# Another order for TensorE, ScalarE and VectorE behind the opening of a fused attention and squared-ReLU kernel

## The chip, the cores and the metric

The kernel runs on one core of one Trainium2 chip. The metric is the device time of one execution in microseconds (us); the median of three executions stands for a version.

## The reference

Four batches of eight heads, 768 positions, 64 values a head. A query sees the 96 positions up to itself and the first 8 positions; the bias falls with the distance, by a slope for each head. The result goes through a layer with a squared ReLU.

```python
scores = scale * q @ k.T                       # per batch and head, 768 x 768
keep   = is_global | is_local                  # pos < 8, or 0 <= i - j < 96
scores = where(keep, scores - slope[h] * dist, -1e9)
a = softmax(scores);  o = a @ v                # (4, 8, 768, 64)
x = o.transpose(0, 2, 1, 3).reshape(3072, 512)
h = maximum(x @ w_in, 0)                       # w_in 512 x 2048
out = (h * h) @ w_out                          # w_out 2048 x 512, out 3072 x 512 f32
```

## The kernel before, in words

The 3072 rows are worked on in eight **halves** of 384 rows (half a batch each). For each half the kernel does, in tiles of 128 rows:

- loads of q, k and v by POOL (L396, cast to 16 bits on the way), and from the third half on a turn of q and k by DMA on SP's queue (`turn_by_dma`, L567);
- **scores** (`score_unit`, L610): matmuls with 64 rows for one or two tile pairs, two PSUM banks a unit; then the exponential on ScalarE (`ex`, L623) and the product with the mask of biases on VectorE (`phat`, L647);
- **attend** (L671): phat times v, with a column of ones that gives the sum; the normalisation on VectorE (`rec` L679, `tm` L681); and, from the third half on, a turn by DMA into `xt` (`to_x_by_dma`, L696, SP's queue), one for each of four pairs of heads;
- **layer 1**: x times w_in, plain (`layer1`, L717) or for some columns by a scheme with seven products in place of eight (`layer1_group`, L841), which needs sums of quarter matrices of x on VectorE (`x_mix`, L818) and keeps partial results (`kept`, L256 and L258; added to the product by L901); then the square (L924 on ScalarE; L926 and L760 on VectorE);
- **layer 2**: the squared rows times w_out, plain (`layer2`, L978) or in the same seven-product scheme for pairs of row tiles (`layer2_pair`, L1064), with sums of rows on VectorE (`mixed`, L1029), results handed out by `y` (L1126, L256, L258), and a store on SP's queue (L1149).

One half's attention is woven into the matrix products of the half before. No scheduler runs when the kernel is built: the table `ORDER` (from L52) is the order. A word names a job and its engine: `p` TensorE (by its number in TensorE's list), `a` ScalarE, `d` VectorE, `s` SP, `g` POOL, `l` a load on POOL's queue. The digits behind a point are the PSUM banks that the job takes, the number behind `+` is a filler, and `@` sets a load behind a DMA. `a` and `d` words name entries of one list of operations, so that writing `a596` as `d596` moves a copy from ScalarE to VectorE. `Plan.run` emits the words one after the other; each engine then works through its own words strictly in that order, and waits where an input, a bank or a buffer is not free:

```python
for word in ORDER.split():
    ...
    op = lists.get(word[0], self.rest)[int(word[1:])]
    self.now, self.spare = [int(i) for i in banks], int(spare or 0) / 100
    op.result = op.emit("POOL" if word[0] == "l" else self.LETTERS[word[0]])
```

Of the kernel before, what the change touches and what calls it, by code (L numbers as in the profile page):

```python
# [51 lines left out]
ORDER = """a4 d1 g2 p0.0 a6 s8 d12 a0 s10 d13 l3 l1 a18 l2 d15 d19 a26 d16 d3 l5 a30 d14 a20 a27 d9 l4 a23  # L52
d5 a22 d17 p1.12+31 a21 l0 p5.34 d11 a7 p10.56 l6 a28 p3 a24 l10 a31 d32 l9 a33 p6 d34 p4.7 a39
l7 p11 d37 a29 p9.0 p8.1 a46 l8 p2.23 d43 a40 p19.7 d35 l11 a47 p7 d55 a25 p13.51 d36 l13 a41
d44 p14.4 p12.67 d48 p15 a42 l12 d59 p17 a49 p16.0 p22.2 d45 l14 p24.4 a52 d51 p23.36 a50 d38
p34.50 l16 d58 a53 p21.7 d64 p25.2 a60 l18 p27.1 d65 a57 p20.4 a61 p32.37 d66 a81 d56 p31.2 l15
a73 p29.6 d68 p18.5 d72 p28.4 a74 p26.3 l19 p36.1 d54 a69 p35.2 p30.7 a86 d70 p33.54 d85 a71 d91
p39.16 a67 p40.27 a77 d63 p37.3 a82 d75 l17 a78 d62 p41.5 a92 d79 d76 p38.0 d84 d80 p45.4 d83
l21 a97 p48.1 d96 a101 l20 a98 p44.2 a89 p47.5 d107 l23 p46.7 a112 p42.0 d111 a108 d110 a93
p43.2 d109 p53.1 a87 p52.5 d102 p50.4 p49.7 a113 l22 d120 d100 a90 d105 p59.6 l27 a116 d119 a103  # L60
d106 p55.3 p51.1 l29 d94 a122 a88 d128 p65.2 l28 a104 d95 a117 p64.4 a118 p58.5 a129 a136 d114
p60.0 d99 a137 l30 d146 d191 p54.3 l24 p62.6 d115 d205 l25 p57.1 a133 p56.4 d125 d121 p63.7
p67.6 a123 d134 d135 a130 d206 p61.1 p72.3 a126 d132 p69.4 d189 a124 p77.7 a131 d156 p70.0 a142
p82.1 d157 d165 a159 p71.5 a160 p74.4 d162 l34 a166 d201 a163 p83.6 d147 a161 l26 p73.0 a167
d522 d164 a138 p84.3 l31 d158 d148 a168 a169 p79.52 d186 l35 a139 d202 p89.04 p81.1 d127 a198
l33 d151 p85 a187 d170 a178 d523 p86 a174 d207 a199 d184 p78.06 a179 d149 l32 p80.57 p88.41 d180
p87 a195 l36 d200 a175 p76.2 d203 a185 l37 d155 p75.4 a196 d193 p91.0 l38 a188 d143 s194 d197
p66.1 a181 l39 d172 a171 p95.3 d152 a173 p90.5 d223 p100.4 d153 a209 s224 a176 d236 p92 d204
p103.2 d177 d208 p68.3 d237 s216 a244 a140 d210 p93.6 d240 a211 p94 a182 d150 s217 a144 d219
p96.1 p104 d225 p97 d183 a245 d221 p98.7 s220 d239 a218 p102.3 d238 p111 d214 d228 s226 l44 p106  # L70
d222 d243 l43 d213 p109.61 s229 d227 p110.73 d154 p99 l40@217 a255 d258 s215 d141 p101 a256
l42@217 d145 a251 d272 d190 p113 l45 a252 a234 p114.73 d254 l41@217 d192 p108.61 p105.0 a248 l46
d246 a261 p107 d253 d259 a262 l47 d257 s260 p115.62 a249 s235 d230 p116.74 l48 p118.3 a264 d250
p131.1 a265 d232 d263 p117.6 a268 d231 a292 p122.2 d266 a273 p121.7 d233 a269 d212 p125.1 a271
d280 s324 p124 d284 p127.4 a283 p126 d241 a278 d267 p123.6 d285 a293 p137.1 s325 d281 p119.5
a287 p132 a286 p129.7 a279 d294 p130 p140 d323 a301 p142 d270 p134.6 a290 d274 a307 p128.1 a291
p135 d288 p133.2 a308 p136 d298 p141.5 a310 d300 s242 a299 p143.1 s282 a297 d309 p139 d326 p138
d524 p112 d395 l50@325 a305 s275 d311 p120 a303 l56 d306 a312 s289 d295 a302 p146.36 l53 p147.54
d304 p145.71 a330 s296 d313 l51@325 a333 p144.2 a331 d318 l52 p148.3 a334 d319 a276 l49@325
p149.5 d321 a327 a322 d433 d332 a328 l54 p151.64 p150.07 d314 p152 d320 a338 l57 d329 p159.1  # L80
a339 l55 p157.0 d336 a337 p172.7 a341 d340 p153 a352 d370 a342 p160.3 a350 d315 p169.6 s371 d353
a344 p158.7 p162 d351 p161 p154.4 d316 a355 d397 p166.3 a347 p164.7 d356 p163 s398 p156 d317
d358 d359 a366 p171.1 d343 p165 s399 p167 a360 d362 p181.7 a363 d335 a361 p170 d345 p175 d367
p177 a357 p174.0 d375 p173.5 a378 d373 p178.3 s247 s277 d369 p176 a383 s354 p180 d368 a372
p155.0 d349 a379 p168.1 a376 d382 a384 d400 p179 p183 l58@399 a364 p182.7 d380 a348 p184 s374
a377 l65 d385 p185.3 a389 l62 a387 d381 s386 p188.41 a365 d388 p187.05 l59@399 p186.27 a405
p189.6 d401 a409 l63 a413 d402 p190.0 a406 d416 l73 a410 d403 p191 a407 l61 d396 a414 p193.42
d412 a417 p194.65 l60@399 d411 a418 p192.71 p195 a422 d415 a419 l64 d391 p200.4 d429 a420 p206.7
d437 a426 p198.0 d392 p219.1 s438 d393 a434 d408 a427 p207.6 p204.4 d394 a447 s346 d489 p210
d443 a462 p202.5 a451 d428 p199.1 a423 d404 p211 a441 p213 d435 p197.4 p217.2 a432 d456 p205.5  # L90
s436 p218.1 d424 a444 d452 p196 d480 s491 a445 d476 a461 d460 p203.6 p215.7 d442 p223 a458 p221
d425 a453 p208 d421 s492 p209 d481 p220 a448 d483 p222.1 a469 d477 p214 a446 d467 p227.6 s390
# [1514 lines left out]
```

## Time and profile before

| | |
|---|---|
| three executions | 199.65, 199.69, 200.62 us; median 199.69 |
| profiled execution | 200.43 us, of which the span of instructions is 198.7 |
| TensorE | busy 191.6 us, 96% of the span, 2381 matmuls |
| weight loads | busy 163.2 us, 82% |
| VectorE | busy 176.3 us, 89%, 450 instructions |
| ScalarE | busy 151.0 us, 76%, 321 instructions |
| turns into xt by DMA | 24, from issue to landing 2.3 to 7.0 us, median 3.0 |
| granted TensorE clock | 1.00 |

In the profile PE is TensorE (PEld its weight loads), DVE VectorE, ACT ScalarE, SP and POOL the queues that issue DMAs; L671 is line 671 of the kernel. Times count from the start of the span. "x24" is a number of instructions, and the name behind an arrow in square brackets is what ended the idle time before the row. Rows of TensorE overlap, since a matmul's results are still draining when the next one streams.

### The profile page before, as it was taken

What the parts mean: (1) busy time and instruction counts of PE and PEld (TensorE: products, weight loads), DVE (VectorE), ACT (ScalarE), POOL (GpSimd) and SP (SyncE); (2) the same over time, 40 slices, a digit from 0 to 9 for tenths busy, and PEclk for the clock granted to TensorE, in tenths of its full rate; (3) what the DMA queues carried; (4) which work ended last, traced back from release to release, by engine and by line L of the source; (5) the groups of instructions that cost most, each with busy time, mean ns of one, the idle gap of its engine ahead of it and who ended that gap; (6) DMA issues with size and microseconds to landing.
All of it is one profiled execution on the core that took longest, in us unless ns stands there. A gap on an engine that the chain in (4) does not pass through costs nothing.

```text
span 198.7 us, 5980 instructions
## 1 busy us (share of the span) xinstructions
PE 191.6 (96%) x2381; PEld 163.2 (82%) x2381; DVE 176.3 (89%) x450; ACT 151.0 (76%) x321; POOL 66.9 (34%) x82
## 2 busy tenths in 40 slices
PE   7798999999999999999999999999999999999993
PEld 3576899856888687788888998999889999999993
DVE  7589696899999999999989999899899996978971
ACT  6799797899555888976999679878897578769211
POOL 8996565187108701940194007800000000000000
PEclk9999999999999999999999999999999999999999
DMA  5999999999999998999899799996531221201214
GB/s 152 182 150 194 189 180 172 209 195 155 182 192 92 155 205 218 107 127 145 218 118 153 104 222 129 161 175 147 102 102 37 94 57 40 109 0 53 109 53 158
DMA packets 106987, 27.52 MB, mean 139 GB/s; under 512 B 97104, under 2 KB 104016, under 8 KB 106960
## 3 DMA queue, kind: packets, MB, share of 16 engines
q0 software_dynamic: 74944, 13.11, 90.1%
q1 hardware_dynamic: 30816, 13.45, 31.7%
q10 hardware_dynamic: 1200, 0.59, 1.1%
q8 instruction: 18, 0.29, 0.6%
q14 instruction: 9, 0.07, 0.1%
HBM read 27.26 MB, written 6.29 MB: 169 GB/s over the span
## 4 chain that ended last, share of the span: by engine, by line
PE 78%; DMA 7%; POOL 5%; DVE 5%; ACT 3%; issue 1%; POOLq 0%; DVEq 0%
PE yps L1064 32%; PE hps L841 19%; PE hps L717 14%; PE sp L610 4%; DMA xt<-tm 4%; DMA w_mix<-in_k_dram 4%; PE av L671 3%; PE yps L978 3%; POOL w_mix L396 2%; POOL v L396 1%; DVE hr L901 1%; ACT h L758 1%; PE av L1380 1%; PE trp L549 1%; DVE vb L258 1%
## 5 line engine op out<-in xcount | busy, mean ns | idle before, releaser
L623 ACT ACTIVATE ex<-sp 128x512 f16<-128x512 f32 x66 | 36.7, 632 | 3.6 <-PE sp L610 3.5
L1064 PEld LDWEIGHTS <-h 128*128 128x128 f16 x376 | 33.9, 98 | 4.0
L717 PE MATMUL hps<-xt,w_in_sb 128*128 128x128 f16 (+2 forms) x288 | 35.6, 273 | 0.3 <-ACT ex L1350 0.3
L256 ACT COPY kept<-hps 128x384 f32<-128x384 f32 x52 | 24.6, 490 | 12.4 <-PE hps L841 8.8
L901 DVE CUSTOM_DVE_ANT_0 hr<-hps,kept 128x384 f16<-128x384 f32 x58 | 30.3, 548 | 1.0 <-PE hps L841 0.6
L717 PEld LDWEIGHTS <-w_in_sb 128*128 128x128 f16 x288 | 23.5, 98 | 5.9 <-DMA w_in_sb<-in_moe_w_in_dram 0.5
L1064 PEld LDWEIGHTS <-mixed 128*128 128x128 f16 x272 | 25.2, 98 | 3.6 <-DVE mixed L1029 0.2
L396 POOL DMA_DIRECT2D sq<-in_q_dram x19 | 17.3, 910 | 31.0 <-DMA q<-sq 23.4
L256 ACT COPY y<-yps 128x256 f32<-128x256 f32 (+2 forms) x39 | 14.6, 385 | 15.8 <-PE yps L1064 15.8
L396 POOL DMA_DIRECT2D sk<-in_k_dram x19 | 17.1, 903 | 24.9 <-DMA q<-sq 22.4
L841 PEld LDWEIGHTS <-w_in_sb 128*128 128x128 f16 x288 | 24.4, 98 | 1.0
L841 PEld LDWEIGHTS <-in_mix 128*128 128x128 f16 x272 | 22.8, 98 | 1.1 <-issue 0.3
L841 PE MATMUL hps<-x_mix,in_mix 128*128 128x192 f16 x204 | 23.4, 246 | 0.0
L1064 PE MATMUL yps<-w_mix,h 128*128 128x256 f16 (+1 forms) x192 | 22.4, 264 | 0.0
L1064 PE MATMUL yps<-w_mix,mixed 128*128 128x256 f16 (+1 forms) x184 | 22.2, 268 | 0.0
L396 POOL DMA_DIRECT2D v<-in_v_dram x24 | 21.8, 922 | 1.2 <-DVE h L760 0.6
L1064 PE MATMUL yps<-w_out_sb,h 128*128 128x256 f16 (+1 forms) x184 | 21.9, 268 | 0.0
L924 ACT ACTIVATE h<-hr 128x768 f16<-128x768 f16 x25 | 20.9, 857 | 0.0
L647 DVE TENSOR_TENSOR phat<-ex,mask 128x1024 f16<-128x1024 f16 (+1 forms) x36 | 20.6, 590 | 0.1
L744 ACT ACTIVATE hr<-hps 128x384 f16<-128x384 f32 (+1 forms) x35 | 18.5, 546 | 2.8 <-PE hps L717 2.8
L841 PE MATMUL hps<-xt,w_in_sb 128*128 128x192 f16 x172 | 19.8, 246 | 0.0
L1126 DVE TENSOR_TENSOR y<-yps,y 128x256 f32<-128x256 f32 (+1 forms) x30 | 11.9, 408 | 3.5 <-PE yps L1064 2.9
(110 smaller groups left out, 354.1 us busy)
## 6 DMA issues: line engine op xcount, KB each, us to landing
out_dram<-y SPq DMA_DIRECT2D x23, 256.0 KB, 2.6
v<-in_v_dram POOLq DMA_DIRECT2D x24, 128.0 KB, 7.1
sq<-in_q_dram POOLq DMA_DIRECT2D x19, 128.0 KB, 6.4
sk<-in_k_dram POOLq DMA_DIRECT2D x19, 128.0 KB, 6.4
w_in_sb<-in_moe_w_in_dram POOLq DMA_DIRECT2D x4, 512.0 KB, 11.0
w_out_sb<-in_moe_w_out_dram POOLq DMA_DIRECT2D x4, 512.0 KB, 12.3
y<-in_q_dram SPq DMA_DIRECT2D x2, 256.0 KB, 4.4
y<-in_k_dram ACTq DMA_DIRECT2D x2, 256.0 KB, 5.1
```

The costliest lines, as they stand in the source:

```text
L256: nc.scalar.copy(out=out, in_=in_)
L396: dma = nc.gpsimd.dma_start(out=dst, in_=src[x.b, :, r0 + t * P:r0 + (t + 1) * P, :] .rearrange("h p d -> p h d"))
L610: nc.tensor.matmul(sp[h][:, i, :], lhsT=lhsT, rhs=x.q[rows, r % HT, a, :], start=True, stop=True)
L623: nc.scalar.activation(out=st["ex"][:, h], in_=sp[h], func=AF.Exp, scale=scale)
L647: eng(e).tensor_tensor(out=x.phat[a][:, :, t0:t0 + n], op=ALU.mult, in0=st["ex"][:, :, i0:i0 + 2 * n].rearrange("p e (t b) c -> p e t (b c ...
L717: nc.tensor.matmul(st["ps"][:, i * n:(i + 1) * n], lhsT=w_in_sb[:, kk, m * P:(m + 1) * P], rhs=x.xt[:, kk, c0:c1], start=kk == 0, stop=kk ...
L744: nc.scalar.activation(out=o, in_=i, func=AF.Relu)
L841: nc.tensor.matmul(st[name][:, i * HC:(i + 1) * HC], lhsT=left(i, kk), rhs=right(kk), start=fresh and i == kk == 0, stop=kk == KK - 1, ski ...
L901: eng(e)._custom_dve(dve_ops.TENSOR_ADD_SAT, out=hidden(which)[:, :, cols], in0=sums(name), in1=st[kept], s0=3.4e38, s1=0.0)
L924: nc.scalar.activation(out=h2, in_=hr, func=AF.Square)
L1064: nc.tensor.matmul(st[bank_name][:, 0:n], lhsT=a(m), rhs=b(m)[:, cols], start=fresh and m == 0, stop=m == HK - 1, skip_group_check=not fresh)
L1126: eng(e).tensor_tensor(out=y, in0=ps, in1=y, op=ALU.add)
```

## The change

The table `ORDER` is replaced by another with the same words. SP's 66 words, POOL's and the 76 loads keep their order. TensorE's 383 jobs stand as before up to the 74th, and so do the last 37; of the jobs between, 235 have another place, by up to 28 places. ScalarE's first 72 and VectorE's first 76 words are the same (but for those that change engines, all of them later); 33 operations go from ScalarE to VectorE and 33 from VectorE to ScalarE, most of them copies (`kept`, `y`), squares and ReLUs. Many jobs take other PSUM banks, in the opening too. A place where the table first differs:

```diff
-p82.1 d157 d165 a159 p71.5 a160 p74.4 d162 l34 a166 d201 a163 p83.6 d147 a161 l26 p73.0 a167
...
+d157 p82.7 d165 a159 p71.4 a160 p74.2 a166 d162 l34 d201 a127 p75.3 d208 a186 d147 l26 p73.0
...
```

The first place is VectorE's queue at 80 to 87 us of the profile before. The rows go from the normalisation of the fourth half's last pair (`tm_1754`) to the mask product `phat_1883`, which the fifth half's first attend reads; `mixed` and `h2` are sums of rows and squares, `x_mix_1868` a sum over the turned fourth half. Before:

```order
L679 RECIPROCAL rec_1752<-av_1681 128x6
L681 TENSOR_TENSOR tm_1754<-av_1681,rec_1752 128x2x3x64
L926 TENSOR_TENSOR h2_1499<-hr_1699 128x768
L760 TENSOR_TENSOR h2_1499<-hr_1719 128x768
L1029 TENSOR_TENSOR mixed_1807<-h2_1499 128x1024
L1029 TENSOR_TENSOR mixed_1820<-mixed_1807,h2_1499 128x1024
L1029 TENSOR_TENSOR h2_1499<-h2_1499 128x8x128
L405 MEMSET v_1841 128x48
L630 TENSOR_TENSOR phat0_1844<-ex_1790,mask_85 128x1024
L818 TENSOR_TENSOR x_mix_1868<-xt_1716 128x384
L1029 TENSOR_TENSOR mixed_1878<-h2_1499,mixed_1820 128x1024
L647 TENSOR_TENSOR phat_1883<-ex_1835,mask_85 128x2x512
```

Now, where the same normalisation gives `tm_1737` and the same product is `phat_1843`:

```order
L679 RECIPROCAL rec_1735<-av_1701 128x6
L681 TENSOR_TENSOR tm_1737<-av_1701,rec_1735 128x2x3x64
L926 TENSOR_TENSOR h2_1507<-hr_1673 128x768
L926 TENSOR_TENSOR h2_1507<-hr_1633 128x768
L760 TENSOR_TENSOR h2_1507<-hr_1671 128x768
L760 TENSOR_TENSOR h2_1507<-hr_1699 128x768
L1029 TENSOR_TENSOR mixed_1796<-h2_1507 128x1024
L647 TENSOR_TENSOR phat_1808<-ex_1774,mask_85 128x2x512
L1029 TENSOR_TENSOR mixed_1812<-mixed_1796,h2_1507 128x1024
L647 TENSOR_TENSOR phat_1843<-ex_1781,mask_85 128x2x512
L405 MEMSET v_1860 128x48
L630 TENSOR_TENSOR phat0_1866<-ex_1794,mask_85 128x1024
```

The mask product now stands ahead of `phat0`, the sum `x_mix` and the last two sums of rows, and another mask product stands ahead of it; the normalisation stands ahead of two squares that it followed.

The second place is TensorE's queue at 143 us, where the eighth half's scores begin. `sp_3117` and `sp_3118` are the banks of its third unit. Before, the unit follows the second one's scores:

```order
L610 LDWEIGHTS kb_1840
L610 MATMUL sp_3108<-q_3013,kb_1840 128x128
L610 LDWEIGHTS k_1839
L610 MATMUL sp_3117<-q_3013,k_1839 128x128
L610 LDWEIGHTS k_1839
L610 MATMUL sp_3118<-q_3013,k_1839 128x128
```

Now the same unit has the banks `sp_3259` and `sp_3260`:

```order
L841 LDWEIGHTS in_mix_800
L841 MATMUL hps_3122<-x_mix_3128,in_mix_800 128x192
L610 LDWEIGHTS k_1858
L610 MATMUL sp_3259<-q_3012,k_1858 128x128
L610 LDWEIGHTS k_1858
L610 MATMUL sp_3260<-q_3012,k_1858 128x128
```

It has moved back and stands by itself, with layer 1 (L841) ahead of it and behind it.

The third place is VectorE's queue where the seventh half's last turned pair is summed. Before, the pair's normalisation `tm_3003` stands 21 rows ahead of the first `x_mix` row; the rows up to the second one that reads the turned half are:

```order
L1029 TENSOR_TENSOR mixed_3169<-h2_2331,mixed_3144 128x1024
L647 TENSOR_TENSOR phat_3184<-ex_3127,mask_85 128x2x512
L647 TENSOR_TENSOR phat_3216<-ex_3139,mask_85 128x2x512
L1029 TENSOR_TENSOR mixed_3222<-h2_2690 128x1024
L1126 TENSOR_TENSOR y_3155<-yps_3146,y_3155 128x256
L818 TENSOR_TENSOR x_mix_3237<-xt_2965 128x384
L258 COPY vb_1842<-v_1841 128x520
L1126 TENSOR_TENSOR y_3182<-yps_3078,y_3182 128x256
L818 TENSOR_TENSOR x_mix_3237<-xt_2965,x_mix_3237 128x384
```

Now the pair's normalisation is `tm_3067`, and the row that waits for its turn is the second `x_mix` row:

```order
L681 TENSOR_TENSOR tm_3067<-av_3048,rec_3065 128x2x3x64
L258 COPY vb_1861<-v_1860 128x520
L258 COPY yps_3001<-y_2861 128x256
L926 TENSOR_TENSOR h2_2732<-hr_3032 128x768
L926 TENSOR_TENSOR h2_2732<-hr_3044 128x768
L818 TENSOR_TENSOR x_mix_3128<-xt_2952 128x384
L926 TENSOR_TENSOR h2_2732<-hr_2908 128x768
L1029 TENSOR_TENSOR mixed_3149<-h2_2732 128x1024
L258 COPY kept_3152<-hps_3122 128x384
L258 COPY y_2861<-yps_3001 128x256
L647 TENSOR_TENSOR phat_3168<-ex_3109,mask_85 128x2x512
L818 TENSOR_TENSOR x_mix_3128<-xt_2952 128x384
```

The pair's attend has moved back on TensorE, behind three groups of layer 2, and ten rows now lie between its normalisation and the sum that reads the turn.

More of the change, by code (lines that the diff above doesn't have):

```diff
@@ L57 @@
[L57 to L62, printed above, removed]
@@ L69 @@
[L69 to L74, printed above, removed]
@@ L75 @@
[L75 to L92, printed above, removed]
@@ L117 @@
[L117 to L120 removed]
+ORDER = """a4 s8 g2 d1 a6 p0.0 l3 s10 d12 d13 a0 l1 a18 l2 d15 d19 a26 d16 a30 l5 d3 a20 a27 d14 d9 a23 l4
+a22 d5 a21 d17 p1.12+31 l0 d11 a7 p5.34 l6 a28 p10.56 a24 l10 p3 a31 d32 l9 a33 d34 p6 l7 p4.7
@@ L123 @@
+a763 p382 s764 d775 s776 a777 a778"""
 class Op:
```

103 lines of the change are left out of this document (65 added, 38 removed).

## The prediction

> **What bounds the kernel now.** I read the page first, then busy time by stretches, then TensorE's own timeline, and last the DMA and VectorE rows beside its late places.
>
> ```profile
> span 198.7 us, 5980 instructions
> PE 191.6 (96%) x2381; PEld 163.2 (82%) x2381; DVE 176.3 (89%) x450; ACT 151.0 (76%) x321; POOL 66.9 (34%) x82
> PE 78%; DMA 7%; POOL 5%; DVE 5%; ACT 3%; issue 1%; POOLq 0%; DVEq 0%
> ```
>
> TensorE is busy for 96% of the span and holds 78% of the chain that ended last, so a new order can only win what TensorE waits. Where it waits, the stretches tell (the columns are length, busy time and instructions of each engine, granted clock, DMA share, rate):
>
> ```profile
> core 0: us, PE busy (x) PEld busy (x) DVE busy (x) ACT busy (x) POOL busy (x), PEclk, DMA share, GB/s
> 0.00:20.00 20.00, 16.34 (x241) 11.45 (x241) 15.94 (x52) 16.46 (x38) 17.45 (x25) 1.00 1.80 170
> 20.00:38.00 18.00, 17.93 (x240) 16.38 (x241) 14.62 (x44) 14.69 (x30) 9.01 (x11) 1.00 1.76 185
> 38.00:195.40 157.40, 157.11 (x1903) 135.32 (x1901) 145.59 (x356) 119.63 (x255) 40.41 (x46) 1.00 1.12 129
> 195.40:198.70 3.30, 0.23 (x5) 0.06 (x2) 0.12 (x1) 0.27 (x1) 0.00 (x0) 1.00 0.40 131
> 80.00:95.00 15.00, 14.72 (x194) 12.55 (x193) 14.50 (x34) 11.48 (x26) 6.45 (x8) 1.00 2.17 123
> 135.00:160.00 25.00, 25.00 (x324) 22.95 (x322) 23.61 (x55) 19.87 (x42) 0.00 (x0) 1.00 0.39 101
> ```
>
> Of the visible idle time, 3.66 us (20.00 - 16.34) lies in the first 20 us and 3.07 us behind the last matmul. TensorE's order first differs with the job that starts at 39.8 us; from 38 to 195.4 us only 0.29 us of 157.40 is idle. The clock is at full speed throughout, so nothing is to be won there.
>
> A busy TensorE can still be late, because one matmul's row overlaps the next. So I compared the distance from start to start with the usual one of the shape. The usual distances are in the chain's rows below (ten of L671 in 0.30, four of L717 in 0.65):
>
> ```profile
> 54.86 0.20 PE L671 MATMUL av<-vb,phat 128*128 128x65 f16 x1
> 55.01 0.27 PE L1064 MATMUL yps<-w_out_sb,mixed 128*128 128x256 f16 x1
> 86.07 0.19 PE L671 MATMUL av<-v,phat 128*128 128x65 f16 x1
> 86.48 0.27 PE L671 MATMUL av<-v,phat 128*128 128x65 f16 x3 [0.22 <-DVE phat L647]
> 92.66 0.65 PE L717 MATMUL hps<-xt,w_in_sb 128*128 128x384 f16 x3
> 93.38 0.41 PE L841 MATMUL hps<-xt,in_mix 128*128 128x192 f16 x3
> 158.76 0.19 PE L671 MATMUL av<-vb,phat 128*128 128x65 f16 x1
> 158.88 0.49 PE L841 MATMUL hps<-xt,w_in_sb 128*128 128x192 f16 x4
> 58.58 2.62 PE yps L1064 x24
> 61.20 0.55 PE sp L610 x16
> 61.75 2.73 PE yps L1064 x24
> 100.48 0.78 PE sp L610 x24
> 106.21 0.65 PE hps L717 x4
> 132.92 0.87 PE yps L1064 x8
> 134.13 0.30 PE av L671 x10
> 133.80 0.33 PE hps L841 x4
> ```
>
> From 54 us on there are ten such late places. The first is at 55.01 (0.15 after its forerunner instead of 0.03, so 0.12 late) and the last at 158.88 (0.09). The two large ones are at 86.48 (0.41 instead of 0.03: 0.38) and at 93.38 (three matmuls at 0.16 from 92.66 end at 93.15: 0.23). The other eight lie between 0.06 and 0.17 and make 0.85; all ten make 1.46 us. This is the cake.
>
> A visit to the scores costs something too: 24 score matmuls take 0.78 and 16 take 0.55, so eight are 0.23 and 16 would be 0.46. That leaves 0.09, and the 24 matmuls of L1064 beside a visit take 2.73 instead of 2.62. A visit thus costs 0.20 beyond its matmuls.
>
> **The change part by part.** Matmuls, copies and DMAs stay the same in number and kind, so TensorE's work is the same. SP's and POOL's orders do not change, so no DMA is moved past another on its queue; when one goes out depends on the work that it waits for.
>
> *Opening, up to 38 us: 0.* The order is kept and only some PSUM banks are renamed. The waits there are for loads. Bounds: the largest late place between 20 and 38 us sits in a stretch with 0.07 idle, so 0.1 either way.
>
> *The two large places: -0.61.* Both lie in 80 to 95 us, where VectorE is busy for 14.50 of 15.00 us and the matmul waits for a VectorE result whose own inputs were long there. VectorE's rows of that time:
>
> ```profile
> 80.60 0.56 DVE L681 TENSOR_TENSOR tm<-av,rec 128x384 f16<-128x384 f32 x1
> 81.07 0.55 DVE L926 TENSOR_TENSOR h<-hr 128x768 f16<-128x768 f16 x1
> 81.54 0.55 DVE L760 TENSOR_TENSOR h<-hr 128x768 f16<-128x768 f16 x1
> 82.20 0.69 DVE L1029 TENSOR_TENSOR mixed<-h 128x1024 f16<-128x1024 f16 x1
> 82.92 0.69 DVE L1029 TENSOR_TENSOR mixed<-mixed,h 128x1024 f16<-128x1024 f16 x1
> 83.53 0.68 DVE L1029 TENSOR_TENSOR h<-h 128x1024 f16<-128x1024 f16 x1
> 85.74 0.69 DVE L647 TENSOR_TENSOR phat<-ex,mask 128x1024 f16<-128x1024 f16 x1
> 86.34 0.42 DVE L1126 TENSOR_TENSOR y<-yps,y 128x256 f32<-128x256 f32 x1
> 88.28 0.36 DVE L818 TENSOR_TENSOR x_mix<-xt,x_mix 128x384 f16<-128x384 f16 x1 [0.23 <-DMA xt<-tm]
> ```
>
> The product of 85.74 is what TensorE waits for at 86.48. In the new order it stands ahead of the sum of 83.53 and all that followed this up to 85.74 (2.21 us by their starts); one other product, 0.60 from start to start (85.74 to 86.34), now stands ahead of it. It comes about 1.6 us earlier, against a lateness of 0.38. The copy that 93.38 waits for (kept, L258) goes to ScalarE, which has 3.5 us idle in that stretch. The turn of the fourth half's last pair, which holds VectorE up for 0.23 at 88.28, is also sent earlier: its normalisation (80.60) stands ahead of two squares (L926, 0.47 each by 81.07 to 81.54) that it stood behind. I count both places as gone. Bounds: -0.61 if nothing else is late next, 0 if the mixed sums that now come later are waited for in their turn (each has some 1.5 us less room).
>
> *The eight short places: 0.* Each is a result that came 0.06 to 0.17 late. All eight consumers stand elsewhere now, so they go; but the new order is woven as tightly, and results that come just in time are as frequent in it by its queues' work. 33 operations go from ScalarE to VectorE and 33 the other way, so neither gets slack. Bounds: -0.85 (all go, none come) and +0.85 (twice as many); I take the middle.
>
> *One more visit to the scores: +0.20.* The eight score matmuls of the eighth half's third unit stand by themselves between two groups of L841, where they followed others before. Nothing hides this, since TensorE is the bound. Bounds: 0.09 (only the exit) to 0.22.
>
> *The end: 0.* The last 37 jobs of TensorE keep their order, and the copies and stores behind the last matmul are the same.
>
> Sum: -0.61 + 0.20 = -0.41 us. The profiled execution took 200.43 us, 1.7 of it outside the span, and the sum would bring it to 200.0. It lies 0.74 above the median of the three runs, 199.69, and nothing tells where; since the sum is a difference, I take it from the median: **199.3 us**. If the 0.74 were late places that the median run does not have, less is to be won.
>
> One rule speaks for a larger cake. The Trainium skill, Perfetto Trace Analysis, section Identifying the Most-Contended Engine, says that matmul busy time is a bad measure of how near TensorE is to its limit, and that the busy share of weight loads is a good one. By it, 157.40 - 135.32 = 22 us would be open behind 38 us. The rows differ: eight matmuls of 256 columns take 0.87 at the rate of one every 0.109 us while loads pause between them, so the pauses in the loads are no open time.
>
> **The rivals.**
>
> *All short places go as well.* The same mechanism carried further: 199.69 - 0.61 - 0.85 + 0.20 = 198.4 us. For it: the order no longer has any of the ten consumers behind the same producer at the same distance. Against it: VectorE has 145.59 us of work in 157.40, and an order of such density has never been free of short waits in this trace.
>
> *Slower: the seventh half's last turn comes late.* One pair of that half (attend, L671, then a turn by DMA, L696) is moved back. Its rows before, and the landings of all such turns:
>
> ```profile
> 135.23 0.49 PE L841 MATMUL hps<-xt,w_in_sb 128*128 128x192 f16 x4
> 148.88 0.35 DVE L818 TENSOR_TENSOR x_mix<-xt 128x384 f16<-128x384 f16 x1
> L696 SPq DMA_TRANSPOSE xt<-tm x24: 1178/1207/2148, 51.7 to 164.3; - x24
> DMA to landing us min/median/max: 2.3/3.0/7.0
> ```
>
> Before, 13.6 us lie between the end of its matmuls (135.23) and the first sum that reads the turned half (148.88). Now the matmul that needs it stands 6.4 us behind it by the chain's prices: four groups of L841 (1.32), four of L1064 (3.48), and visits of 24 and 16 scores with their entries (0.89 and 0.66). Its way takes 1.2 (normalisation 0.8, part of two sums of 0.42 ahead of it), the landing, and two x_mix rows with their hand-over (0.8): 5.0 with the median of 3.0, and 9.0 with 7.0, which is 2.6 late and gives 201.9 us. It costs from a landing of 4.4 us on and ends over 200.7 from 5.8. Against it: the landing of 7.0 fell into 80 to 95 us with a DMA share of 2.17, and at this place the share is 0.39. VectorE itself reaches the x_mix row only some 5.4 us after those matmuls (ten rows, 4.4 us from start to start, behind the normalisation), so about 0.4 us of room is left even with a quick landing.
>
> *Slower: twice as many short places.* 199.69 + 0.85 + 0.20 = 200.7 with the two large ones replaced by equals.
>
> *It does nothing.* What leaves 80 to 95 us is waited for a few microseconds later: 199.7 to 199.9.
>
> *Denser matmuls.* By the weight loads' pauses some of 22 us; even a tenth would be 197.5. The rows of 0.87 and 0.33 speak against it.
>
> **How the numbers follow.** A measurement of this kernel can tell about 0.5%, 1.0 us, from no change. The forecast (199.3) has 0.50, nothing (199.8) 0.15, all short places gone (198.4) 0.18, denser matmuls 0.01, the late turn 0.08, twice as many short places 0.08. Faster by over 0.5%: 0.19; within: 0.65; slower: 0.16. The range goes from 198.3 (the first rival with 0.1 from the opening) to 201.0 (the bounds of the sum, 200.7, and a part of the late turn); it leaves out most of the late turn and the tails.
>
> **What would show it.** Behind 38 us, the late places sum to about 0.9 us instead of 1.46, none above 0.3 between 80 and 95 us; TensorE visits the scores once more there, with 0.2 us around eight matmuls; the row x_mix that waits for a landing at 88.28 waits no more; the clock stays at full speed and the opening and the end keep their rows. I am wrong if a late place over 0.5 us appears, above all in front of L841 near 147 us, or if the opening moves.

## The result, and the profile after

| | before | after |
|---|---|---|
| executions side by side, median | 199.95 us (9, 199.59 to 200.62) | 200.85 us (9, 200.64 to 201.80) |
| ratio, 95% interval | | 1.0057 (1.0037 to 1.0077) |
| profiled execution, span | 200.43, 198.7 | 200.85, 199.1 |

The new order is slower by 0.9 us by the medians, 1.1 by the ratio. A second comparison later gave 1.0041 (1.0015 to 1.0067). The page of the changed kernel reads almost as before; in the chain of waits, transfers have grown from 7% to 14%:

```profile
span 199.1 us, 5962 instructions
PE 191.3 (96%) x2381; PEld 163.2 (82%) x2381; DVE 177.0 (89%) x449; ACT 149.6 (75%) x322; POOL 67.0 (34%) x82
PE 79%; DMA 14%; POOL 5%; issue 0%; ACT 0%; POOLq 0%
```

Busy time by stretches of the changed kernel (columns as in the prediction):

```profile
38.00:195.83 157.83, 156.95 (x1903) 135.72 (x1900) 146.16 (x355) 117.98 (x256) 40.55 (x46) 1.00 1.10 129
80.00:95.00 15.00, 15.00 (x194) 12.67 (x189) 14.07 (x34) 11.93 (x25) 7.88 (x9) 1.00 2.00 142
67.00:83.00 16.00, 15.14 (x177) 11.33 (x175) 13.79 (x34) 14.20 (x31) 4.53 (x6) 1.00 1.44 165
```

and the last of these stretches in the kernel before:

```profile
67.00:83.00 16.00, 16.00 (x200) 12.27 (x195) 15.20 (x41) 14.17 (x31) 5.83 (x8) 1.00 1.57 177
```

From 80 to 95 us TensorE now has no idle time (0.28 before), so the two large late places are gone. From 67 to 83 us it has 0.86, where before it had none. TensorE's timeline of the changed kernel shows where: the fifth half's first scores stand 1.50 us behind a row of three matmuls at 0.16, so 1.01 late.

```profile
78.14 0.65 PE L717 MATMUL hps<-xt,w_in_sb 128*128 128x384 f16 x3
79.64 0.34 PE L610 MATMUL sp<-q,k 64*128 64x128 f16 x6 [0.85 <-DMA q<-sq]
```

They wait for the turn of q. SP's row of this turn, and the landing times of all ten turns of q and k, in the changed kernel:

```profile
72.34 4.30 SPq L567 DMA_TRANSPOSE q<-sq  x1
DMA to landing us min/median/max: 3.7/4.4/7.2
```

and before:

```profile
72.56 3.31 SPq L567 DMA_TRANSPOSE q<-sq  x1
DMA to landing us min/median/max: 3.6/4.9/6.1
```

Before, this turn landed at 77.94 and the scores came at 80.45, 2.5 us later. These 2.5 us are called the room of the landing here: by so much it could come later without a wait. In the new order the scores stand ahead of two L978 jobs that they followed (four matmuls of 512 columns each, 1.7 us together), and the order is 0.36 us ahead at 67 us: nearly all of the room was gone. The turn was issued 0.2 us earlier and still landed 1.6 us later, at 79.50, the 7.2 us of the row.

Where both orders have done the same TensorE jobs, their times can be compared. The lengths of the stages between such places, from the start of the first matmul behind each (before: 36.36, 67.35, 82.13, 105.59, 141.13, 173.42, last matmul 195.41 us):

| stage of before, us | before | after | after, 2nd profile | after, 3rd profile |
|---|---|---|---|---|
| 36 to 67 | 30.99 | 30.63 | 30.61 | 30.63 |
| 67 to 82 | 14.78 | 16.14 | 16.18 | 15.86 |
| 82 to 105 | 23.46 | 22.81 | 22.80 | 22.81 |
| 105 to 141 | 35.54 | 35.44 | 35.87 | 35.48 |
| 141 to 173 | 32.29 | 32.30 | 32.30 | 32.30 |
| 173 to the last matmul | 21.99 | 22.16 | 22.17 | 22.17 |

Between 67 and 82 us 1.36 us are lost, more than the whole; another 0.17 is lost behind 173 us, and the other stages gain or stay.

### The profile page after: what moved, and what is told of

Read it like the earlier page. It is cut to its first block, busy times and chain, and to the rows that moved or that the text cites. A ratio compares the mean times of both kernels' runs of the same rounds, so it can differ in the third digit from the quotient of the medians.

```text
span 199.1 us, 5962 instructions
## 1 busy us (share of the span) xinstructions
PE 191.3 (96%) x2381; PEld 163.2 (82%) x2381; DVE 177.0 (89%) x449; ACT 149.6 (75%) x322; POOL 67.0 (34%) x82
## 4 chain that ended last, share of the span: by engine, by line
PE 79%; DMA 14%; POOL 5%; issue 0%; ACT 0%; POOLq 0%
PE yps L1064 34%; PE hps L841 23%; DMA w_in_sb<-in_moe_w_in_dram 10%; PE hps L717 9%; PE sp L610 4%; PE yps L978 4%; DMA q<-sq 4%; PE av L671 3%; POOL w_mix L396 3%; POOL v L396 1%; PE trp L549 1%; POOL sq L396 1%; POOL sk L396 0%; PE av L1380 0%; POOL far L294 0%
## 5 line engine op out<-in xcount | busy, mean ns | idle before, releaser
L623 ACT ACTIVATE ex<-sp 128x512 f16<-128x512 f32 x66 | 36.1, 622 | 2.3 <-PE sp L610 2.3
L901 DVE CUSTOM_DVE_ANT_0 hr<-hps,kept 128x384 f16<-128x384 f32 x58 | 30.9, 549 | 2.1 <-PE hps L841 1.6
L256 ACT COPY y<-yps 128x256 f32<-128x256 f32 (+2 forms) x43 | 16.3, 390 | 21.4 <-PE yps L1064 21.3
L256 ACT COPY kept<-hps 128x384 f32<-128x384 f32 x49 | 22.3, 487 | 8.3 <-DVE hr L901 3.3
L841 PEld LDWEIGHTS <-w_in_sb 128*128 128x128 f16 x288 | 24.2, 98 | 1.6 <-issue 0.2
L841 PEld LDWEIGHTS <-in_mix 128*128 128x128 f16 x272 | 23.3, 98 | 1.3
L841 PE MATMUL hps<-x_mix,in_mix 128*128 128x192 f16 x204 | 23.4, 246 | 0.0
L924 ACT ACTIVATE h<-hr 128x768 f16<-128x768 f16 x24 | 20.0, 851 | 1.2 <-DVE hr L901 1.1
L841 PE MATMUL hps<-xt,w_in_sb 128*128 128x192 f16 x172 | 19.6, 246 | 0.0
```

Of the source, the lines that this page charges most:

```text
L256: nc.scalar.copy(out=out, in_=in_)
L623: nc.scalar.activation(out=st["ex"][:, h], in_=sp[h], func=AF.Exp, scale=scale)
L841: nc.tensor.matmul(st[name][:, i * HC:(i + 1) * HC], lhsT=left(i, kk), rhs=right(kk), start=fresh and i == kk == 0, stop=kk == KK - 1, ski ...
L901: eng(e)._custom_dve(dve_ops.TENSOR_ADD_SAT, out=hidden(which)[:, :, cols], in0=sums(name), in1=st[kept], s0=3.4e38, s1=0.0)
L924: nc.scalar.activation(out=h2, in_=hr, func=AF.Square)
```

## The experiments

The tables below name stages by these places. "Seam" is the place where one order is continued by the other.

### The room given back in front of the scores

```diff
-p117.2 a305 l50@325 d295 a309 p145.56 a271 p147.13 l56 d306 p146.04 s289 a333 p112
-d304 a327 l53 d279 a334 p120 d313
+p117.2 a305 l50@325 d295 a309 p112 p120 p145.56 a271 p147.13 l56 d306 p146.04 s289 a333
+d304 a327 l53 d279 a334 d313
```

> The changed kernel with the two L978 jobs (eight matmuls of 512 columns, 1.7 us by 0.216 each) ahead of the fifth half's first scores again, as in the kernel before. In the changed kernel those scores stood 1.01 us behind their forerunner at 79.64 us, waiting for the turn of q that landed at 79.50. Theory (the lost room of this turn is the loss): the scores come at about 80.3, after the landing; the wait goes, nothing else moves, the time falls by about 1.0 us to 199.9, a ratio to the kernel before of 1.000 (0.998 to 1.002). Rival (the loss is spread over many new short waits, or lies in the opening): the ratio stays near 1.005.

Measured: 1.0083 (1.0052 to 1.0113). The wait for q is gone (landed at 78.75, scores at 80.74), but the second visit to the scores, which now follows the first after 0.98 us of other work, waits in the middle, and the row names an exponential:

```profile
83.02 0.21 PE L610 MATMUL sp<-q,k 64*128 64x128 f16 x1
83.51 0.32 PE L610 MATMUL sp<-q,k 64*128 64x128 f16 x5 [0.28 <-ACT ex L623]
```

These places and those right behind them sum to 1.0 us, 0.6 us of a wait for the turn of xt stands at 67 us, and 0.57 of a wait for VectorE at 124.50. Theory and rival both miss. The two L978 jobs had been the cover for six exponentials; a job moved away from one wait uncovers the next.

### The room taken in the old order

```diff
-d524 p112 d395 l50@325 a305 s275 d311 p120 a303 ... d304 p145.71 a330 s296 d313 l51@325 a333 p144.2
+d524 d395 l50@325 a305 s275 d311 a303 ... d304 p145.71 p112 a330 s296 d313 l51@325 a333 p120 p144.2
```

> The kernel before with the same two L978 jobs moved behind the fifth half's first scores, and nothing else. The scores would come at about 78.7 us instead of 80.45. Theory A (it is the room alone): q lands where it did before, at 77.9, or some tenths later, kb is ready at 78.4, so the wait is 0 to 0.3 us and the ratio 1.000 to 1.002. Theory B (the early scores make the landing late by themselves): q lands near 79.5, the wait is 0.8 us or more and the ratio 1.004 or more. Rival (the place is without effect): no wait in front of L610 in either.

Measured: 1.0042 (1.0024 to 1.0061). q landed at 78.69, the scores came at 79.05 without waiting for it, 1.4 us earlier than before; they waited for banks instead (0.54 us), and 0.35 us of a wait for the turn of xt stands at 67.77:

```profile
79.76 0.21 PE L610 MATMUL sp<-q,k 64*128 64x128 f16 x1
80.14 0.32 PE L610 MATMUL sp<-q,k 64*128 64x128 f16 x5 [0.17 <-ACT hr L744]
```

The stage 82 to 105 became 22.80 instead of 23.46, just as in the new order, and 67 to 82 grew by 0.95. So in this profile the one move brings the gain of the new order in that stage (nothing is waited for at 86 and 93 us) and a loss nearly as large, but not by the same waits: it is 0.54 for banks and 0.35 for xt, and none for q. The time fits neither A's sum (1.002 at most) nor B's reason.

### The instruction packets moved

```diff
-        for _ in range(8):
-            nc.tensor.matmul(ps, lhsT=zero[:, 0:P], rhs=zero, start=True, stop=True)
+        for _ in range(32):
+            nc.tensor.matmul(ps[:, 0:P], lhsT=zero[:, 0:P], rhs=zero[:, 0:P], start=True, stop=True)
```

> The changed kernel with its order untouched; the eight 512-column warm-up matmuls of the opening become 32 of 128 columns (the same 3.4 us by the 0.107 us of the cold 128-column rows), so TensorE has 24 matmuls and 24 weight loads more. The trace of the changed kernel shows an instruction packet of 16 KB at 74.58 us that takes 1.10 us, and 256-byte packets of the q and k turns that then take 1.45 us; in the kernel before it came at 73.34 and fell together with a pause that the turns have anyway. Theory (the late landing comes of the instruction packet falling into the turn): 48 more instructions bring it about 1.9 us earlier (24.9 instructions per us), to 72.7, q lands at 78.4 or earlier instead of 79.50, the wait of 0.85 in front of L610 shrinks to 0 to 0.2, and the time falls by 0.7 to 1.0 us (ratio 0.999 to 1.003). Rival (the landing is late for another reason): q lands at 79.5 as before, the wait stays 0.85, the ratio 1.005.

Measured: 1.0176 (1.0147 to 1.0205), 203.63 us. The packets moved, by 0.6 to 3.4 us (74.58 to 72.4, 61.31 to 57.9, 142.8 to 142.2), and the fifth half's turns, which a packet had hit, landed within 5.1 and 4.8 us instead of 6.8 and 7.2. But they were issued 2.0 to 2.2 us later, behind loads that had waited for the fourth half's q turn (landed at 61.03 instead of 60.10). That turn was now hit, and so was the eighth half's. TensorE waits for both:

```profile
61.17 0.23 PE L610 MATMUL sp<-q,k 64*128 64x128 f16 x2 [0.41 <-DMA q<-sq]
144.15 0.23 PE L610 MATMUL sp<-q,k 64*128 64x128 f16 x2 [0.93 <-DMA q<-sq]
```

The second is the cleanest case. The eighth half's q turn lands 3.6 to 3.8 us after its issue in 19 profiles of 20; here a packet came at 142.2 while it was under way, and it took 5.3. The landing times go with the packets as the theory said, the forecast time doesn't: a packet moved out of one turn falls into another.

### One product ahead, in the old order

```diff
-p149.5 d321 a327 a322 d433 d332 a328 l54 p151.64 p150.07 d314 p152 d320 a338 l57 d329 p159.1
+p149.5 d321 a327 a322 d433 d332 a328 d329 l54 p151.64 p150.07 d314 p152 d320 a338 l57 p159.1
```

> The kernel before with one VectorE instruction moved: the product phat (L647) that TensorE waits for at 86.48 us stands ahead of the sum x_mix and of one mixed sum (0.35 and 0.68 us), right behind the exponentials it reads (84.70). Theory of the prediction (the late place comes of VectorE's order): the product comes at about 84.9 instead of 85.74, the 0.38 us at 86.48 goes, and the time falls by up to 0.4 (ratio 0.998 to 1.000). Rival: another result is late at the same place or just behind it, and the time stays (1.000).

Measured: 1.0018 (0.9996 to 1.0039). The product comes at 84.59 instead of 85.74, but the sum x_mix that it passed is now late (0.44 us), and L841, which reads it, waits:

```profile
84.59 0.69 DVE L647 TENSOR_TENSOR phat<-ex,mask 128x1024 f16<-128x1024 f16 x1
85.20 0.35 DVE L818 TENSOR_TENSOR x_mix<-xt 128x384 f16<-128x384 f16 x1
```

```profile
85.69 0.49 PE L841 MATMUL hps<-x_mix,in_mix 128*128 128x192 f16 x4 [0.28 <-ACT ex L623]
```

The row names the exponential, which ended at 85.56; the sum ended at 85.55, and only the sum was moved (before, L841 went at 85.41 while that exponential still ran). The rival holds: VectorE's order alone doesn't free this place.

### The changed kernel once more

> The changed kernel, untouched, profiled once more. Theory: the wait in front of the fifth half's first scores (0.85 us at 79.64) belongs to this order, since the scores stand 1.7 us earlier than before and q landed between 77.9 and 79.5 in all six profiles so far: q lands between 78.5 and 79.6 and the wait is 0.2 to 0.9 us. Rival (a stray of one execution): q lands before 78.4 and the wait is gone, with the time still near 200.8.

Measured: 201.27 us, no ratio (one execution). q landed at 78.74, where the theory had it, and still is not waited for, which was the rival's sign; but the time isn't better, because another turn was late, that of the third half's last pair into xt (issued at 61.04, landed at 67.72, 6.7 us; in the first profile 5.6):

```profile
66.95 0.25 PE L841 MATMUL hps<-xt,w_in_sb 128*128 128x192 f16 x1
67.77 0.41 PE L841 MATMUL hps<-xt,w_in_sb 128*128 128x192 f16 x3 [0.57 <-DMA xt<-tm]
```

0.73 us here and 0.22 at the next sum. The fifth half's scores came at 79.65 as in the first profile. So the wait in front of these scores isn't in every execution of the order; the stage is as long (16.18 instead of 16.14), by a wait for another landing.

### The two visits spaced as before

```diff
-p117.2 a305 l50@325 d295 a309 p145.56 ... p112 ... p120 ... p144.2 a331 d335 l52 a328 d319 p151.15 a276 p150.30 l49@325 p157.4 d329 a341 p148.6 a338 d433 l54 a322 d332 p149.7
+p117.2 a305 l50@325 d295 a309 p112 p120 p145.56 ... p144.2 p148.5 p149.7 a331 d335 l52 a328 d319 p151.16 a276 p150.30 l49@325 p157.4 d329 a341 a338 d433 l54 a322 d332
```

> The changed kernel with the fifth half's two visits to the scores spaced as in the kernel before: the two L978 jobs ahead of the first visit (as in the first experiment), and the two L1064 products of 0.87 us (p148, p149) between the first visit and the second, which wait there for nothing that the exponentials make; two banks swap names behind. Theory (the loss is the lost room at both ends: in front for the landing of q, behind for six exponentials of 0.48): neither wait appears, TensorE reaches the end of this stage 0.8 to 1.0 us earlier than in the changed kernel, ratio 0.998 to 1.001. Rival (other places of the new order take the loss): the ratio stays at 1.004 or above.

Measured: 1.0191 (1.0178 to 1.0205). Neither of the two waits is there. But ScalarE's queue was left as it was, and the copy that the moved products wait for stands behind exponentials in it (1.57 us here, 0.94 at 87.6):

```profile
84.83 0.60 PE L1064 MATMUL yps<-w_mix,mixed 128*128 128x256 f16 x4 [1.41 <-ACT y L256]
```

It tells nothing on theory or rival, only that TensorE's jobs can't be moved without ScalarE's.

### New order to 82 us, then old; and the reverse

The tables were joined behind the product p144.

> The new order up to the product behind the fifth half's first scores (p144, at 82 us), the old order from there on; banks renamed so that each job keeps its bank across the seam. By the profiles the new order is 1.0 us behind at that visit and gains 0.65 between 79 and 104 us. Theory (the loss lies ahead of 82 us): ratio 1.003 to 1.006. Rival (the loss lies behind 82 us): ratio 0.998 to 1.001.

Measured: 1.0097 (1.0062 to 1.0131). Again a turn of q was late, that of the fourth half (landed at 62.02, in 17 of the 20 profiles at 59.6 to 60.2), 1.24 us, and the fifth half's as well, 0.37. The sign is the theory's, the size larger.

> The old order up to the same product, the new order from there on, with p148 and p149 between the two visits as in the old order. Theory (the new order is better behind 82 us, by the 0.65 us of the profiles, less 0.17 at 176 us): ratio 0.996 to 0.999. Rival (it is no better there): 1.000 or above.

Measured: 1.0056 (1.0043 to 1.0068). Here p148 and p149 had been moved as in the experiment on spacing, with the same flaw (0.94 us of waits for ScalarE's copies), so it doesn't decide. Up to 82 us the stages are the old ones (31.03 and 14.77).

### The same at 104 us

The seam lies behind p195, and no job is moved.

> The old order up to the product p195 (104 us), the new order from there on; at this seam both orders have done the same TensorE jobs, and banks are renamed so that each job keeps its bank. Theory (the loss lies ahead of 104 us, in landings that come late): only the lone visit (0.2 us) and the x_mix wait at 176 us (0.17) of the new order remain, ratio 1.000 to 1.002. Rival (the loss lies behind 104 us): 1.004 or above.

Measured: 1.0061 (1.0037 to 1.0086), as the rival said. In its profile 0.79 us is a wait for the turn of xt at 68.26, in the old order, and 0.91 lies at 107 to 108 us, right behind the seam, where neither order alone has it. The seam itself costs too much here for a verdict.

> The new order up to the same seam at 104 us, the old order from there on. Theory (the loss lies ahead): ratio 1.003 to 1.006, with 0.6 us or more of waits for landings between 60 and 82 us. Rival (the loss lies behind): 0.998 to 1.001.

Measured: 1.0028 (1.0006 to 1.0050), just under the theory's range. Its profile has 1.27 us of a wait for the turn of xt at 68.09 (landing 7.0), 0.22 behind it, and nothing above 0.14 after 74 us.

### Less traffic

```diff
-        for word in ORDER.split():
+        for word in [w for w in ORDER.split() if w not in ("s260", "s235")]:
...
-                dma = nc.gpsimd.dma_start(out=dst, in_=src[x.b, :, r0 + t * P:r0 + (t + 1) * P, :]
-                                          .rearrange("h p d -> p h d"))
+                dma = nc.gpsimd.memset(dst, 0.5) if (name, x.hb) == ("v", 4) else nc.gpsimd.dma_start(
+                    out=dst, in_=src[x.b, :, r0 + t * P:r0 + (t + 1) * P, :].rearrange("h p d -> p h d"))
```

> The changed kernel with the order of TensorE, ScalarE and VectorE untouched and less traffic between 60 and 75 us: the three loads of v of the fifth half (128 KB each) become fills on GpSimd, and the two stores of y at 66 us (256 KB each) are left out, so output and one half's values are not the reference's. Theory (the loss is waiting for landings that come later than the new order needs them): the turns of k and q are issued at about the same time and land 1.5 us or more earlier (before 78.0), no wait of over 0.3 us is left in front of the scores near 61 and 79 us and of L841 near 67 us, and the time falls by 0.7 us or more against the changed kernel: ratio to the kernel before 1.002 or below. Rival (the new order waits for its own engines): 1.004 or above.

Measured: 1.0064 (1.0039 to 1.0090). The turn of q lands at 77.56, 0.8 to 2.8 us earlier than in the other profiles of the new order up to there, and isn't waited for. But the turn of xt, which was issued ahead of the traffic left out, took 7.4 us, and the wait moved there:

```profile
68.24 0.41 PE L841 MATMUL hps<-xt,w_in_sb 128*128 128x192 f16 x3 [1.23 <-DMA xt<-tm]
```

The theory's landing of q holds, its time doesn't. The time is the rival's, its reason isn't: the wait is for a landing, not for the kernel's own engines.

> The kernel before with the same traffic left out (three loads of v of the fifth half, two stores of y). Theory (the old order has room for these landings already): the time stays within 0.3 us, ratio 0.998 to 1.001. Rival (all orders gain from lighter traffic alike): the ratio falls by as much as that of the changed kernel with the same traffic left out, 0.995 to 0.997.

Measured: 1.0018 (0.9998 to 1.0038); the turns of k and q land at 75.49 and 76.79 instead of 76.59 and 77.94, and TensorE gains nothing by it; its profile has 0.50 us of a wait at 81.23, and the row names a normalisation on VectorE. That speaks for the theory's room and against the rival, but the ratio lies just above the theory's range.

### Smaller moves of the instruction packets

In the new order and in the old one, the five warm-up matmuls ahead of the first transposes are left out:

```diff
-p1.12+31
+p1.12
```

> The changed kernel without the five warm-up matmuls ahead of its first transposes (ten instructions less on TensorE), its order untouched. The 16 KB instruction packets then come about 0.4 us later against the transfers: the one at 61.0 to 61.3 us some 0.3 to 0.8 us behind the issue of the turn of xt at 60.9. Theory (the packet's place sets this landing): the turn lands within 4.9 to 6.1 us, before 67.0, the wait in front of L841 at 67 us is 0.3 or less, and the ratio to the kernel before is 1.003 or below. Rival (the landing scatters by itself): lands anywhere from 5.6 to 7.4, ratio 1.005 or above.

Measured: 1.0027 (1.0008 to 1.0047). The packet didn't move as meant: it came at 60.68, earlier, 0.13 us ahead of the turn's issue, and the turn took 7.0 us, in the profile 1.14 us of wait. Its 11 runs form two groups, 199.88 to 200.23 (four) and 200.81 to 201.20 (six), with one between; the profiled one is of the upper. The ratio is in the theory's range, for a reason that it didn't give. The rival's landing fits, its ratio doesn't.

> The kernel before without the same five warm-up matmuls. Its packet at 61.0 to 61.6 us comes about 0.4 us later. Theory: the turn of xt lands within 6.1 us of its issue, TensorE does not wait at 67 us, and the executions in which it did (two of six profiles of the old order up to there) become rarer: ratio 0.997 to 1.000. Rival: no change, 1.000, or a loss in the opening by a colder TensorE, above 1.001.

Measured: 0.9987 (0.9968 to 1.0005); 11 of 12 runs between 199.39 and 199.90. Here too the packet came early, at 61.04 instead of 61.58, and the turn took 6.4 us for a wait of 0.15, more than the theory's 6.1. The ratio is in the theory's range, and no change lies in its interval as well.

In the new order, four of the eight warm-up matmuls were cut up:

```diff
-        for _ in range(8):
-            nc.tensor.matmul(ps, lhsT=zero[:, 0:P], rhs=zero, start=True, stop=True)
+        for n in [512] * 4 + [P] * 16:
+            nc.tensor.matmul(ps[:, 0:n], lhsT=zero[:, 0:P], rhs=zero[:, 0:n], start=True, stop=True)
```

> The changed kernel with four of the eight warm-up matmuls of 512 columns cut into sixteen of 128 (24 instructions more on TensorE in the same time), its order untouched. The instruction packets come about 0.96 us earlier, the one at 61.0 to 61.3 at 60.1 to 60.4, half a us ahead of the issue of the turn of xt. Theory (the packet's place sets the landing): it overlaps the first packets of that turn, or the last of the q turn that lands at 60.1, and one of the two is late: 0.6 us or more of waits between 60 and 68 us, ratio 1.006 or above. Rival (the landing scatters by itself): ratio near 1.005.

Measured: 1.0089 (1.0068 to 1.0111). The packet came at 59.39 and fell into the fourth half's q turn, which landed at 61.41 (59.6 to 60.2 in 17 profiles); TensorE was 0.99 us late in front of its scores:

```profile
61.55 0.23 PE L610 MATMUL sp<-q,k 64*128 64x128 f16 x2 [0.82 <-DVE v L405]
```

The row names a VectorE fill that is no input of these matmuls; what they read and what landed last is q. As the theory said.

### New order to 67 us, then old

> The new order up to the first product behind the turn of xt (p118, 67 us), the old order from there on, banks renamed by their first use. The new order reaches this place 0.36 us earlier (30.63 instead of 30.99 us from 36 us). Theory (landings bound this stage): TensorE waits for the turn of xt by as much, and the gain is given back: ratio 1.000 to 1.003. Rival (order bounds it): the gain stays, ratio 0.997 to 0.999.

Measured: 1.0018 (0.9991 to 1.0045). The first stage keeps its gain (30.63), and the next one takes 15.28 instead of 14.78, with 0.33 us of a wait for a sum over the turned xt at 70.41 and 0.19 for a kept copy at 71.27. The gain of 0.36 is given back and the ratio is in the theory's range, but its reason isn't seen: the turn of xt landed at 66.40 and TensorE doesn't wait for it.

### The changed kernel, and the old one with fewer warm-ups, again

> The changed kernel, untouched, once more with a third profile. Theory (landings near 60 to 80 us that the new order has no room for, late in most executions and in time in some): a median of 200.6 to 201.2 with runs in two groups some 0.8 us apart, and in the profile 0.5 to 1.5 us of waits for a turn of xt or of q between 60 and 82 us if its time is above 200.6, none over 0.3 if it is below 200.3. Rival (a loss that every execution has): no run below 200.4, and a profile whose waits between 60 and 82 us don't go with its time.

Measured: 1.0041 (1.0015 to 1.0067). Seven of the 12 runs lie from 199.91 to 200.47, one at 200.82, four from 201.51 to 202.41: groups, as the theory said, though further apart, and with a median of 200.45 below its 200.6. But the profiled run, of the lower group (200.27), has 0.73 us of a wait for q at 79.03 (landed at 78.90), so this wait by itself doesn't make the difference between the groups. What the upper group has more was not seen.

> The kernel before without the five warm-up matmuls, once more, since its first comparison (0.9987, interval 0.9968 to 1.0005) left open whether it is faster than the kernel before. If it is: ratio 0.996 to 0.999 again with an interval below 1. If not: 0.999 to 1.002.

Measured: 0.9984 (0.9960 to 1.0007). Both comparisons of this version lie below 1 and both intervals reach 1; that it beats the kernel before isn't shown. No version is clearly faster than the kernel before.

### All profiles together

Stages in us, of the profiles in which the engines' order of that stage is the old or the new one without an edit and without a seam at its start, the instruction packets not moved by 24 rows or more (the two runs with less traffic are in; the room taken in the old order is left out up to 105 us, its 22.80 would make the old mean of 82 to 105 us 23.17):

| order | 36 to 67 | 67 to 82 | 82 to 105 | 105 to 141 |
|---|---|---|---|---|
| old | 30.57 to 31.03 (7), mean 30.87 | 14.77 to 15.67 (7), mean 14.99 | 22.96 to 23.46 (6), mean 23.23 | 35.44 to 35.66 (8), mean 35.54 |
| new | 30.63 (9), 31.77 (1), mean 30.74 | 15.49 to 17.02 (7), mean 16.29 | 22.80 to 22.81 (6), mean 22.81 | 35.44 to 36.07 (8), mean 35.63 |

New minus old by the means: -0.13, +1.30, -0.42, +0.09, and +0.17 behind 173 us, together +1.0; measured were 1.1 (1.0057) and 0.8 (1.0041).

Of the +1.30, 0.35 stands in every profile of the new order: at 71.10 (0.18 late, a copy of y) and 72.24 (0.17, a kept copy), both for ScalarE. The rest is landings: in the seven profiles 1.01 (q), 0.95 (xt), 0.73 (q), 1.49 (xt), 1.61 (xt), 1.36 (xt) and 0.37 (q), mean 1.07, against 0.79 (xt), 0.15 (xt) and five times less than 0.1 in the old order.

The third half's last turn into xt and the instruction packet next to it, in 17 profiles whose next loads went out 0.2 to 0.7 us ahead of this turn:

| packet, against the issue of the turn | profiles | issue to landing |
|---|---|---|
| 0.14 us ahead to at once | 7 | 6.3 to 7.4 us |
| 0.16 behind | 1 | 6.4 |
| 0.37 to 0.54 behind | 9 | 4.9 to 6.1 |

In the other three the packet had come 2 to 3.5 us earlier and hit the q turn; the loads then went out behind the turn of xt, and it landed in 2.4 to 3.4 us. There both causes are mixed. They are in part mixed in the table as well: all eight turns over 6.2 us have loads that went out 0.56 to 0.68 us ahead. But of the eleven with such loads, the three whose packet came 0.48 to 0.54 behind landed in 4.9 to 6.1 us, the other eight in 6.3 to 7.4.

## Why the prediction was wrong

**The step that failed** is the sentence "SP's and POOL's orders do not change, so no DMA is moved past another on its queue". No transfer was moved past another, but TensorE's jobs were moved towards transfers that had stayed. The sum had no term for the room between a landing and its first reader, so the stage from 67 to 82 us stood in it at nothing; it became 1.36 us longer in the profile (16.14 instead of 14.78), 1.30 by the means. The kernel before showed the room: landing 77.94, scores at 80.45. Taking 1.7 us for the two L978 jobs and 0.36 for the gain ahead of 67 us leaves 0.4 us for q. At 67 us there was less: the third half's last turn into xt landed at 67.14, and the second matmul of L841, at which the wait stands in the other profiles, came at 67.44; the same 0.36 takes all of it. With landings of q and k that spread from 3.6 to 6.1 us in the same trace, that is a loss to be counted. Of the seven profiles of the new order here, three waited for q and four for xt, 1.07 us on average; the 0.35 for ScalarE's copies belong to the short places.

The time lies inside the range that the prediction gave, and that is luck: its upper end was made of twice as many short places and of a late turn of the seventh half, and neither came. Of the 1.55 us between the forecast and the time, 0.26 is the median that it started from, 199.69 of three executions; nine have 199.95.

- *Opening 0*: right. Both stand at 36.36.
- *Two large places, -0.61*: gone; the product comes at 83.41 instead of 85.74, no sum waits for the turn of 88.28 any more, and the stage 82 to 105 is 0.65 shorter in the profiles predicted from, 0.42 by the means. The reason was half wrong. The prediction laid it on VectorE's order; moving the product alone left 0.44 at the same place, while moving the two L978 jobs alone gave the whole stage. So the gain was not to be had without moving those jobs, in what was tried here.
- *Eight short places, 0*: behind 38 us, without the wait for q, the short places that are not entries and exits of visits sum to 0.8 to 0.9 in the changed kernel, near the forecast (the largest are 0.18, 0.17, 0.18 and 0.17, at 71.10, 72.24, 132.02 and 176.58).
- *One more visit, +0.20*: 0.10 at its entry and 0.12 at its exit, 0.22. It stands at 149.69; four matmuls of 0.082 behind 149.26 would end at 149.59.

```profile
149.26 0.49 PE L841 MATMUL hps<-x_mix,in_mix 128*128 128x192 f16 x4
149.69 0.23 PE L610 MATMUL sp<-q,k 64*128 64x128 f16 x2
```

- *Late turn of the seventh half (0.08)*: it didn't come; its last turn landed within 3.7 us, under the 4.4 from which it was to cost, and the rows from 146.74 to 149.26 follow without a gap. Its mechanism came at two other places. The prediction priced a late landing for one turn of the 24 into xt and for none of the ten of q and k.
- *Twice as many short places (0.08)*: its 200.7 is nearest to the time, with another cause.
- *"I am wrong if a late place over 0.5 us appears"*: 1.01 at 79.64.

Shown is where the time went (the stages), that it is waits for landings and 0.35 of ScalarE's, and that moving the two L978 jobs alone gives both the gain and a loss. Not shown is that the lost room is all of it: no version that gave the room back became faster, since each uncovered another wait. The room alone doesn't make the four waits for xt: 0.36 us in each would be 0.2 us of the mean. In these four the turn also landed later, at 67.72 to 68.19 instead of 65.70 to 67.26 in six of the seven profiles of the old order, with a packet 0.04 to 0.14 us ahead of its issue each time; whether the new order brings the packet there is open. Not shown either is why the fifth half's q turn took 7.2 us instead of 5.4 (in the third profile the packet came at 73.33, as in the kernel before, and it took 6.9), nor why runs of the changed kernel fall into two groups.

## What to carry to other kernels

When an order is changed, list for each transfer the landing and its first reader, and subtract what the reader moves ahead; where the rest is smaller than the spread of the landings in the trace, it is a price, even though no queue of transfers was touched. A gain on the bounding engine ahead of such a reader takes from the same room. And a job that covers one wait often covers another: moving it back, or its neighbours in one engine's queue alone, only changed the name of the wait here.

## What the hardware showed

Turns by DMA land later where an instruction packet comes at certain moments of them. Every 10 us on average (18 between 14.8 and 185.5 us before) the trace has a packet of 16 KB on a queue of its own; the one near 61 us, with one at the issue of the turn of xt in the second profile of the changed kernel (window 60 to 61 us, columns packets, MB, share):

```profile
q8 instruction: 1, 0.02, 7.5%
```

and one half a us behind it in the kernel before (window 61 to 62 us):

```profile
q8 instruction: 1, 0.02, 5.9%
```

They go with TensorE's instructions: with 24 more matmuls in the opening they came 0.6 to 3.4 us earlier, and there were 19 instead of 18. The number alone doesn't place them: with five fewer, the one near 61 us came earlier too. What goes with them is seen best in the eighth half's q turn of that run. In 141 to 142 us its queue moves 840 packets; with the instruction packet at 142.22 the next window has

```profile
q1 hardware_dynamic: 266, 0.06, 32.5%
```

and the one behind it 134. The kernel before and the changed one, whose packets came behind this turn, have no such break in it behind 139.3 us. In the fifth half's turns a break stands behind the packet of the changed kernel (74.58; window 75 to 76 us) as well as behind that of the kernel before (73.34; window 74 to 75 us), so there the break by itself doesn't tell the late landing from the other:

```profile
q1 hardware_dynamic: 79, 0.02, 207.7%
q1 hardware_dynamic: 71, 0.02, 29.0%
```

How a packet holds up a turn is not shown. It doesn't always: a packet 0.37 to 0.54 us behind the issue of the turn of xt lies in the turn too, and those landed in 4.9 to 6.1 us.

The Trainium skill, Runtime: NRT & Kernel Launch, section Instruction fetch mechanics, says that a sequencer fetches its instructions in blocks of 16 KiB, 256 of them, by a DMA queue of its own, and that the cost of a boundary is mostly hidden. The trace agrees with the block and its pace (two rows for each matmul, 24.5 rows a us, 256 in 10.4 us). It doesn't agree with the cost where a turn is under way that is waited for: 5.3 us to the landing instead of 3.6 to 3.8 for the eighth half's q, and 0.93 us of TensorE's time.

A second thing: the turns of one kernel differ by up to 1.4 us from one execution to the next with nothing changed (in three profiles of the changed kernel the fourth half's turn of k took 4.3, 5.6 and 5.7 us, the fifth half's of q 7.2, 6.2 and 6.9, the third half's last into xt 5.6, 6.7 and 5.7). One profile is one draw of these.
